# A soft-capped attention and spectral mixing kernel: block sums moved behind the first low parts, a script of its own for the first batch, channel weight blocks split one step ahead

## The chip, the cores and the metric

One core of a Trainium2 chip runs the whole program. The metric is the device time of one execution in microseconds. Three runs of the kernel before took 902.58, 902.90 and 904.99 us, so the median is 902.9 us.

## What is computed

Attention over 8 batches, 12 heads, 448 positions and 64 dimensions per head, with scores capped by a tanh, and behind it a mixing stage on the 768 joined channels, all in float32:

```python
scores = scale * (q @ k.T);  scores = cap * tanh(scores / cap)
x = softmax(scores) @ v                      # per head, heads joined to [b, 448, 768]
theta = x @ w_theta
y = w_tok_r @ (x * cos(theta)) + w_tok_i @ (x * sin(theta))
u = x + y
out = u + max(u @ w_ch, 0)
```

## The kernel before

**Slots.** The 96 heads are handled as 48 pairs. The program walks through slots `s`, and slot `s` computes the scores, tanh and exp of pair `s` and the product of the probabilities with `v` of pair `s - 1`. Slots 0 to 7 (`opening`) do that alone; from slot 8 each slot also carries a sixth of the mixing stage of one batch (`slot`, `part_scripts`). Six slots make a batch: slots 8 to 13 mix batch 0, slots 14 to 19 batch 1, up to batch 6; batch 7 is mixed in the lists of `TAIL` after the attention has ended.

**The mixing stage of a batch** has three products on TensorE (PE), each in three passes of high and low parts: `theta` (names `th`, lines 440 to 442) in rows 0 and 1 of the script, the mixing over positions (`mix`, `mx`, lines 505 to 507) in rows 2 and 3, the channel product (`chan`, `ch`, lines 440 to 442) in rows 4 and 5. Each has six blocks of 128 channels. Between `theta` and `mix`, block by block, VectorE (DVE) folds the angle (`fold`, lines 457 to 459), ScalarE (ACT) takes sine and cosine (`sincos`), DVE multiplies with x (`rotate`, line 468) and transposes within squares (`turn`, line 475), two rounds of DMA through a DRAM tile finish the transposition (`turn`, `back`, lines 477 and 483, issued on SP), ACT makes the high part (`high`, `zh`, line 491) and DVE the low part (`low`, `zl`, line 497). `mix` of a block starts with `zh` and needs `zl` at its third matmul. `gain` (line 511) adds the result to x on DVE, `us` splits it for the channel product.

**Sums of the softmax.** `add_half` adds the exponentials of a pair on DVE into `psz` and reduces them over blocks of 32 keys into `part` (lines 304, 306, 294). On every second pair, the odd ones, it also reduces the last keys of both pairs (`rest`, line 294) and adds those to `part` (line 314). `sums` (event `r`) is a small matmul on `part` (line 368), `invert` (event `inv`) the reciprocal `rq` and a DMA to DRAM, `spread` (event `bc`) four DMAs that bring the factors back, `norm` multiplies x with them.

**Weights.** The blocks of `w_theta`, `w_tok` and `w_ch` arrive as 64-bit words and are split on the chip into high and low float32 parts (`Split`, lines 102 to 135): a load on SP into a staging room, a scaling on ACT (`scale`) or DVE (`vscale`, line 121), and six DVE instructions, plus the cast to the high part on ACT or on DVE (lines 126 to 135). The staging room of `ch` blocks 0, 2 and 4 is `g_sb[0]`, that of 1, 3 and 5 `g_sb[1]`; the same two tiles hold blocks 0 to 2 and 3 to 5 of the rotated values, so a channel block can be loaded only after the low parts of those are made. The table `WEIGHTS` says at which slot and position (`a`, `b`, `c`, for the events `wa`, `wb`, `wc`) a step is loaded (`>`), scaled (`*` on ACT, `#` on DVE) and split (no mark).

**Order.** Everything runs in the order in which it is written, on each engine's own in-order queue; SP issues all DMAs but those of `v`. Nothing is rescheduled. The order inside a slot is the row of `part_scripts`, event by event. In the rows, `SA` and `SB` are the two halves of the scores, `V` the product with `v`, `A`, `B` the two exps, `a`, `b` the two halves of the sums (`a-`, `b-` those of the pair of the slot before), `q` the load of the pair two slots ahead. PSUM accumulators of 512 columns rotate through three buffers.

Of the kernel before, what the change touches and what calls it, by code (L numbers as in the profile page):

```python
# [36 lines left out]
def softcap_attn_then_spectral_mix(ctx, tc, qk2, v, vj, cap, w_theta, w_tok, w_ch, sel, outT):  # L37
# [115 lines left out]
    def weight_steps():  # L153
        for m in range(NJ):
            ms = slice(m * P, (m + 1) * P)
            steps["th", m] = Split(room_g(m), w_theta[m], wth_h[:, :, ms], wth_l[:, :, ms])
            steps["ch", m] = Split(room_g(m), w_ch[m], wch_h[:, :, ms], wch_l[:, :, ms], m not in (2, 4))
# [138 lines left out]
    def add_half(k, half):  # L296
# [5 lines left out]
        if joint(k):  # L302
# [5 lines left out]
            if k % 2 == 1:  # L308
                rest = wk.tile([P, 2 * TB], F32, tag="rest", name=f"rest{k}", bufs=1)
                block_sums(rest, ph)  # L310
                part = parts[k] = state.pop("part")
                for n in range(2):
                    rows = slice(n * D, (n + 1) * D)
                    nc.vector.tensor_tensor(part[rows, n], part[rows, n], rest[rows], op=ALU.add)
# [8 lines left out]
        if k % 2 == 1:  # L323
            parts[k] = state.pop("part")

# [200 lines left out]
    def part_scripts(b):  # L526
        return [row.split() for row in (
# [9 lines left out]
        )]  # L537
# [57 lines left out]
    def slot(s):  # L595
# [6 lines left out]
        def do(e):  # L602
# [28 lines left out]
            if e in ("a-", "b-") and tail:  # L631
                add_half(k, "ab".index(e[0]))
            if e == "norm":
# [92 lines left out]
```

## Time and profile before

| what | value |
|---|---|
| runs | 902.58, 902.90, 904.99 us |
| the profiled execution's own time | 905.26 us |
| its span, first to last instruction | 903.5 us |
| busy: PE, PE weight load, DVE, ACT | 98 %, 73 %, 74 %, 66 % |
| mean granted TensorE clock | 0.991 of full |

The span is the time from the first to the last instruction that the profiler saw; the 1.8 us that the own time has more lie around it. Busy shares are means over the whole span: an engine with 74 % can be the limit in one slot and idle in the next. A matmul's duration is modelled and overlaps its neighbours', so the distance between the starts of two matmuls is the better measure of PE's pace.

### The profile page before, as it was taken

What the parts mean: (1) busy time and instruction counts of PE and PEld (TensorE: products, weight loads), DVE (VectorE), ACT (ScalarE), POOL (GpSimd) and SP (SyncE); (2) the same over time, 40 slices, a digit from 0 to 9 for tenths busy, and PEclk for the clock granted to TensorE, in tenths of its full rate; (3) what the DMA queues carried; (4) which work ended last, traced back from release to release, by engine and by line L of the source; (5) the groups of instructions that cost most, each with busy time, mean ns of one, the idle gap of its engine ahead of it and who ended that gap; (6) DMA issues with size and microseconds to landing.
All of it is one profiled execution on the core that took longest, in us unless ns stands there. A gap on an engine that the chain in (4) does not pass through costs nothing.

```text
span 903.5 us, 12561 instructions
## 1 busy us (share of the span) xinstructions
PE 884.3 (98%) x4848; PEld 660.2 (73%) x4848; DVE 668.7 (74%) x939; ACT 592.2 (66%) x596; POOL 1.1 (0%) x7
## 2 busy tenths in 40 slices
PE   8999989999999999999999999999999999999997
PEld 5333757667787787787777877877877777789997
DVE  5998996996975579756878569765797568864851
ACT  6988775457964687666976479746885568754320
POOL 0000000000000000000000000000000000000000
PEclk9999979999999999999999999999999999999999
DMA  7573176412652237232461225522273233501521
GB/s 262 190 216 123 50 213 203 136 68 73 196 152 84 79 98 214 79 113 84 146 190 52 103 72 164 183 74 83 75 211 111 93 104 115 172 22 50 193 84 64
DMA packets 67339, 112.81 MB, mean 125 GB/s; under 512 B 9672, under 2 KB 49096, under 8 KB 67272
## 3 DMA queue, kind: packets, MB, share of 16 engines
q1 hardware_dynamic: 61656, 102.95, 36.0%
q10 hardware_dynamic: 5616, 8.98, 3.4%
q8 instruction: 40, 0.66, 0.3%
q14 instruction: 27, 0.22, 0.1%
HBM read 76.89 MB, written 33.17 MB: 122 GB/s over the span
## 4 chain that ended last, share of the span: by engine, by line
PE 75%; DVE 10%; ACT 7%; DMA 4%; issue 2%; SPq 1%; DVEq 0%; POOL 0%; POOLq 0%
PE mx L507 8%; PE s L239 8%; PE mx L505 8%; PE mx L506 8%; PE a L336 7%; PE ch L440 6%; PE ch L442 6%; PE ch L441 6%; PE th L440 4%; PE th L442 4%; PE th L441 3%; ACT p L268 3%; PE s L228 2%; DMA g_sb<-turn 2%; DVE g_sb L475 2%; PE a L347 2%
## 5 line engine op out<-in xcount | busy, mean ns | idle before, releaser
L268 ACT ACTIVATE p<-s,qscale 128x1792 f32<-128x1792 f32 (+1 forms) x96 | 166.5, 1734 | 135.6 <-PE s L239 107.1
L507 PE MATMUL mx<-wtk_h,zl 128*128 128x448 f32 x336 | 125.2, 372 | 3.1 <-DVE zl L497 3.1
L505 PE MATMUL mx<-wtk_h,zh 128*128 128x448 f32 x336 | 125.6, 374 | 0.0
L506 PE MATMUL mx<-wtk_l,zh 128*128 128x448 f32 x336 | 124.1, 369 | 0.0
L442 PE MATMUL ch<-us,wch_l 128*128 128x448 f32 x288 | 106.1, 368 | 1.9 <-DVE wch_l L135 1.9
L440 PE MATMUL ch<-us,wch_h 128*128 128x448 f32 x288 | 107.4, 373 | 0.2 <-ACT wch_h L131 0.2
L440 PE MATMUL th<-xs,wth_h 128*128 128x448 f32 x288 | 106.7, 370 | 0.0
L441 PE MATMUL ch<-us,wch_h 128*128 128x448 f32 x288 | 105.8, 367 | 0.0
L442 PE MATMUL th<-xs,wth_l 128*128 128x448 f32 x288 | 105.2, 365 | 0.0
L441 PE MATMUL th<-xs,wth_h 128*128 128x448 f32 x288 | 105.2, 365 | 0.0
L280 ACT ACTIVATE p<-p,cap_sb 128x1792 f32<-128x1792 f32 (+1 forms) x56 | 100.1, 1788 | 0.4
L336 PE MATMUL a<-p,v 128*64 128x448 f32 x480 | 99.0, 548 | 0.0
L497 DVE TENSOR_TENSOR zl<-g_sb,zh 128x896 fp32r<-128x896 f32 x48 | 51.5, 1086 | 33.4 <-ACT zh L491 13.9
L519 DVE SCALAR_TENSOR_TENSOR x<-ch,x 128x448 f32<-128x448 f32 x48 | 29.8, 621 | 58.0 <-PE ch L442 58.0
L507 PEld LDWEIGHTS mx<-wtk_h,zl 128*128 128x128 f32 x336 | 63.9, 190 | 12.0 <-DVE zl L497 6.6
L505 PEld LDWEIGHTS mx<-wtk_h,zh 128*128 128x128 f32 x336 | 64.0, 191 | 10.8 <-issue 3.4
L336 PEld LDWEIGHTS a<-p,v 128*64 128x64 f32 x480 | 30.9, 136 | 51.5 <-issue 43.0
L506 PEld LDWEIGHTS mx<-wtk_l,zh 128*128 128x128 f32 x336 | 64.0, 190 | 5.2
L440 PEld LDWEIGHTS ch<-us,wch_h 128*128 128x128 f32 x288 | 54.5, 189 | 9.3 <-issue 3.1
L491 ACT CAST zh<-g_sb 128x896 fp32r<-128x896 f32 x48 | 44.6, 938 | 25.4 <-DMA g_sb<-turn 9.4
L440 PEld LDWEIGHTS th<-xs,wth_h 128*128 128x128 f32 x288 | 54.1, 188 | 9.2 <-issue 5.1
L442 PEld LDWEIGHTS ch<-us,wch_l 128*128 128x128 f32 x288 | 54.6, 190 | 6.7 <-DVE wch_l L135 2.3
(88 smaller groups left out, 1486.6 us busy)
## 6 DMA issues: line engine op xcount, KB each, us to landing
turn<-g_sb SPq DMA_DIRECT2D x48, 448.0 KB, 3.1
g_sb<-turn SPq DMA_DIRECT2D x192, 112.0 KB, 3.2
qk_sb<-in_qk SPq DMA_DIRECT2D x39, 448.0 KB, 3.5
out_dram<-x SPq DMA_DIRECT2D x48, 224.0 KB, 1.9
bc<-inverse SPq DMA_DIRECT2D x80, 112.0 KB, 3.4
v<-in_vj ACTq DMA_DIRECT2D x20, 256.0 KB, 2.6
g_sb<-in_wth SPq DMA_DIRECT2D x6, 768.0 KB
g_sb<-in_wch SPq DMA_DIRECT2D x6, 768.0 KB, 4.7
```

Of the source, the lines that this page charges most:

```text
L239: nc.tensor.matmul(sp[:, i, hh, :S], kk[k][rows, 1, at : at + P], qq[k][rows, 0, :], start=n == 0, stop=n == 2)
L268: return lambda: nc.scalar.activation(pp[rows, :n], sp[rows, :n, :, :S], AF.Tanh, scale=qscale[rows])
L280: nc.scalar.activation(pp[rows], pp[rows], AF.Exp, scale=cap_sb[rows])
L336: nc.tensor.matmul(acc[hh * D : (hh + 1) * D, :S], va[:, c, hh, :], pt[k, c // 2][:, c % 2, hh, :], start=c == 0, stop=False)
L440: nc.tensor.matmul(acc[:, :S], wh[:, j, ms], t[:, 0, :], start=j == 0, stop=False)
L441: nc.tensor.matmul(acc[:, :S], wh[:, j, ms], t[:, 1, :], start=False, stop=False)
L442: nc.tensor.matmul(acc[:, :S], wl[:, j, ms], t[:, 0, :], start=False, stop=j == NJ - 1)
L491: nc.scalar.copy(zh.rearrange("p c (g t) -> p c g t", g=4), turned(j))
L497: nc.vector.tensor_tensor(zl.rearrange("p c (g t) -> p c g t", g=4), turned(j), zh.bitcast(F32).rearrange("p c (g t) -> p c g t", g=4), op ...
L505: nc.tensor.matmul(acc[:, :S], zh[:, c, :], wtk_h[:, c, :], start=c == 0, stop=False)
L506: nc.tensor.matmul(acc[:, :S], zh[:, c, :], wtk_l[:, c, :], start=False, stop=False)
L507: nc.tensor.matmul(acc[:, :S], zl[:, c, :], wtk_h[:, c, :], start=False, stop=c == NC2 - 1)
```

## The change

1. **Sums in two events.** The part of `add_half` that reduces `ph` (`rest`) and adds it to `part` becomes a function `add_ends` with events of its own, `c` and `c-` (for the pair of the slot before).
2. **Rows 1 and 2 of the script (slots 9, 15, 21, ...).** Row 1: `b` moves behind `fold5` (the last event). Row 2: `c-` stands behind `low1`, and `r inv` moves from before `SB` to behind `mix0`. In rows 3 and 5 `c` stands right behind `b`, and the events that are dropped from the rows do nothing there.
3. **The first batch has rows 1 and 2 of its own.** `fold4`, `fold5`, `b-` and `c-` move into slot 10, `r inv bc` there behind `mix1`, and the weight events move.
4. **Channel blocks.** Block 1 is split at (9, `b`) instead of (9, `a`); block 2 is loaded at (10, `b`) and split at (10, `c`), where before it was loaded at (10, `c`) and split at (11, `c`); block 4 goes from (12, `c`) to (11, `c`), block 5 from (13, `b`) to (12, `c`), scaled on DVE. The cast of blocks 1 and 5 goes from ACT to DVE.

```diff
-            steps["ch", m] = Split(..., m not in (2, 4))
+            steps["ch", m] = Split(..., m in (0, 3))
...
-        (8, "b"): "tk5", (8, "c"): "*tk6 *ch1", (9, "a"): "tk6 ch1", (10, "c"): ">ch2", (11, "c"): ">ch3 #ch2 ch2 >ch4", (12, "b"): "*ch3 ch3 >ch5", (12, "c"): "#ch4 ch4", (13, "b"): "*ch5 ch5",
+        (8, "b"): "tk5", (8, "c"): "*tk6 *ch1", (9, "a"): "tk6", (9, "b"): "ch1", (10, "b"): ">ch2", (10, "c"): "#ch2 ch2 >ch4", (11, "c"): ">ch3 #ch4 ch4",
+        (12, "b"): "*ch3 ch3 >ch5", (12, "c"): "#ch5 ch5",
...
             block_sums(state["part"][:, k % 2], psz)
-            if k % 2 == 1:
-                rest = ...; block_sums(rest, ph)
-                ...
+    def add_ends(k):
+        if k % 2 == 0 or not joint(k):
+            return
+        rest = wk.tile([P, 2 * TB], F32, tag="rest", name=f"rest{k}", bufs=1)
+        block_sums(rest, ph)
+        part = parts[k] = state.pop("part")
+        for n in range(2):
+            rows = slice(n * D, (n + 1) * D)
+            nc.vector.tensor_tensor(part[rows, n], part[rows, n], rest[rows], op=ALU.add)
...
-            "SA fold2 norm sincos0 V wa x v r SB tB prep wb rotate0 turn0 rotate1 turn1 back0 rotate2 turn2 back1 q"
-            " A th3 fold3 a B b th4 fold4 back2 wc th5 fold5",
-            "SA high0 low0 high1 sincos1 low1 V wa x v r inv SB tB prep q wb rotate3 turn3 high2 rotate4 turn4 back3 mix0 gain0 low2"
-            " rotate5 turn5 back4 back5 bc A B wc mix1 gain1 mix2",
+            "SA fold2 norm sincos0 V x v SB tB prep rotate0 turn0 rotate1 turn1 back0 rotate2 turn2 back1 q"
+            " A th3 fold3 a B th4 fold4 back2 th5 fold5 b",
+            "SA high0 low0 high1 sincos1 low1 c- V x v SB tB prep q rotate3 turn3 high2 rotate4 turn4 back3 mix0 r inv gain0 low2"
+            " rotate5 turn5 back4 back5 bc A B mix1 gain1 mix2",
...
+        if b == 0:
+            rows[1] = ("SA fold2 norm sincos0 V wa x v SB tB rotate0 turn0 rotate1 turn1 wb back0 rotate2 turn2 back1 q"
+                       " A B th3 fold3 a th4 back2 th5")
+            rows[2] = ("SA high0 low0 fold4 fold5 high1 sincos1 low1 b- c- V x v SB tB q rotate3 turn3 high2 rotate4 turn4 back3 mix0 gain0 low2"
+                       " rotate5 turn5 back4 back5 A B wb mix1 gain1 wc r inv bc mix2")
```

How the queues move, at three places. The first is DVE at the end of slot 10 of batch 0. Before, from `gain1` to the low part of block 3:

```order
L511 TENSOR_TENSOR x_256<-mx_1_1004,x_256 128x448
L304 TENSOR_TENSOR psz<-p_0_901 128x896
L511 TENSOR_TENSOR x_304<-mx_2_1027,x_304 128x448
L497 TENSOR_TENSOR zl_3_1063<-g_sb_94,zh_3_1061 128x896
L497 TENSOR_TENSOR zl_4_1076<-g_sb_94,zh_4_1074 128x896
```

Now, from behind `gain1`, the same stretch:

```order
L121 TENSOR_SCALAR g_sb_93<-g_sb_93 128x768
L126 TENSOR_SCALAR g_sb_93<-g_sb_93 128x768
L127 SCALAR_TENSOR_TENSOR g_sb_93<-g_sb_93 128x768
L128 TENSOR_SCALAR g_sb_93<-g_sb_93 128x768
L129 SCALAR_TENSOR_TENSOR g_sb_93<-g_sb_93 128x768
L133 CAST wch_h<-g_sb_93 128x6x128
L134 TENSOR_TENSOR g_sb_93<-g_sb_93,wch_h 128x768
L135 TENSOR_TENSOR wch_l<-g_sb_93 128x6x128
L411 RECIPROCAL rq_1026<-r_1024 56x32
L305 TENSOR_TENSOR psz<-p_0_889 128x896
L516 TENSOR_TENSOR x_304<-mx_2_1036,x_304 128x448
L502 TENSOR_TENSOR zl_3_1072<-g_sb_94,zh_3_1070 128x896
```

The eight instructions that scale and split channel block 2 (`g_sb_93` is the staging room) and the reciprocal `rq` now stand ahead of the low part of block 3.

The second is SP in slot 10 of batch 0. Before, from the last turn of the batch on:

```order
L477 DMA turn_5_985<-g_sb_94 128x896
L483 DMA g_sb_94<-turn_4_952 32x4x224 x4
L483 DMA g_sb_94<-turn_5_985 32x4x224 x4
L417 DMA bc_995<-inverse_934 64x448 x2
L417 DMA bc_998<-inverse_934 64x448 x2
L114 DMA g_sb_93<-in_wch 128x1536
L190 DMA qk_1091<-in_qk 128x896
```

Now:

```order
L482 DMA turn_5_979<-g_sb_94 128x896
L488 DMA g_sb_94<-turn_4_946 32x4x224 x4
L488 DMA g_sb_94<-turn_5_979 32x4x224 x4
L114 DMA g_sb_93<-in_wch 128x1536 x2
L413 DMA inverse_1028<-rq_1026 56x32
L422 DMA bc_1030<-inverse_1028 64x448 x2
L422 DMA bc_1033<-inverse_1028 64x448 x2
L191 DMA qk_1100<-in_qk 128x896
```

The load of channel block 2 still stands right behind the eight DMAs that bring back blocks 4 and 5; block 4's load follows it, and the four `bc` DMAs and the load of the next pair stand behind both.

The third is DVE around the first low parts of the later batches, here batch 1 (slots 15 and 16). Before:

```order
L306 TENSOR_TENSOR psz<-psz,p_1_1647 128x896
L294 TENSOR_REDUCE part_1581<-psz 128x28
L294 TENSOR_REDUCE rest_1704<-ph 128x28
L314 TENSOR_TENSOR part_1581<-part_1581,rest_1704 64x28 x2
...
L497 TENSOR_TENSOR zl_0_1776<-g_sb_93,zh_0_1774 128x896
L497 TENSOR_TENSOR zl_1_1782<-g_sb_93,zh_1_1778 128x896
L406 RECIPROCAL rq_1803<-r_1801 56x32
...
L511 TENSOR_TENSOR x_558<-mx_0_1840,x_558 128x448
L497 TENSOR_TENSOR zl_2_1863<-g_sb_93,zh_2_1830 128x896
```

Now:

```order
L307 TENSOR_TENSOR psz<-psz,p_1_1647 128x896
L295 TENSOR_REDUCE part_1581<-psz 128x28
L502 TENSOR_TENSOR zl_0_1772<-g_sb_93,zh_0_1770 128x896
L502 TENSOR_TENSOR zl_1_1778<-g_sb_93,zh_1_1774 128x896
L295 TENSOR_REDUCE rest_1780<-ph 128x28
L329 TENSOR_TENSOR part_1581<-part_1581,rest_1780 64x28 x2
...
L411 RECIPROCAL rq_1858<-r_1856 56x32
L516 TENSOR_TENSOR x_558<-mx_0_1834,x_558 128x448
L502 TENSOR_TENSOR zl_2_1863<-g_sb_93,zh_2_1824 128x896
```

The first two low parts now stand ahead of `rest` and its two additions (and the second half of the sums behind both folds), while the set of instructions ahead of the third low part, `zl_2`, is the same as before.

## Rows read from the trace of the kernel before

**Rows 1.** The page: busy time of the engines, and the chain that ended last by engine.
```profile
PE 884.3 (98%) x4848; PEld 660.2 (73%) x4848; DVE 668.7 (74%) x939; ACT 592.2 (66%) x596; POOL 1.1 (0%) x7
...
PE 75%; DVE 10%; ACT 7%; DMA 4%; issue 2%; SPq 1%; DVEq 0%; POOL 0%; POOLq 0%
```
**Rows 2.** Who waited for whom, PE's own list: line, what it waited for, us in total, times, longest.
```profile
PE mx L507 <- DVE zl L497: 3.1, 7, 0.7
```
**Rows 3.** Timeline of PE, batch 0, slots 10 and 11: start, us, line, operands, count, and in brackets the idle time before it and its releaser.
```profile
123.53 0.37 PE L368 MATMUL r<-sel_sb,part 128*56 128x32 f32 x2 [2.96 <-DVE part L314]
...
127.35 0.74 PE L507 MATMUL mx<-wtk_h,zl 128*128 128x448 f32 x1 [0.70 <-DVE zl L497]
...
128.63 0.57 PE L507 MATMUL mx<-wtk_h,zl 128*128 128x448 f32 x1
129.00 0.57 PE L505 MATMUL mx<-wtk_h,zh 128*128 128x448 f32 x1
...
134.03 0.36 PE L505 MATMUL mx<-wtk_h,zh 128*128 128x448 f32 x1
134.23 0.36 PE L506 MATMUL mx<-wtk_l,zh 128*128 128x448 f32 x1
...
142.63 1.74 PE L249 MATMUL s<-qk_sb 64*64 64x448 f32 x16
...
148.88 0.36 PE L507 MATMUL mx<-wtk_h,zl 128*128 128x448 f32 x1
```
**Rows 4.** Timeline of PE, batch 0, slot 13: the first matmuls of channel block 5.
```profile
192.21 0.47 PE L440 MATMUL ch<-us,wch_h 128*128 128x448 f32 x1 [0.16 <-ACT wch_h L131]
...
194.79 0.74 PE L442 MATMUL ch<-us,wch_l 128*128 128x448 f32 x1 [1.91 <-DVE wch_l L135]
```
**Rows 5.** Stretches of 4 us: length, busy us and instructions of PE, PEld, DVE, ACT, POOL, then the granted clock of PE, the DMA share and GB/s.
```profile
120.00:124.00 4.00, 1.04 (x14) 0.43 (x10) 3.87 (x6) 0.94 (x1) 0.00 (x0) 0.89 0.97 257
124.00:128.00 4.00, 3.30 (x12) 1.25 (x13) 3.86 (x8) 3.65 (x4) 0.00 (x0) 0.50 0.65 138
128.00:132.00 4.00, 4.00 (x13) 3.52 (x12) 3.28 (x5) 3.97 (x5) 0.00 (x0) 0.50 0.55 167
132.00:136.00 4.00, 4.00 (x18) 3.68 (x17) 3.18 (x4) 2.35 (x3) 0.00 (x0) 0.83 0.67 246
...
192.00:196.00 4.00, 1.94 (x6) 1.42 (x6) 3.96 (x5) 3.72 (x4) 0.00 (x0) 0.85 0.12 48
196.00:200.00 4.00, 4.00 (x16) 3.32 (x17) 3.93 (x6) 2.16 (x5) 0.00 (x0) 0.73 0.30 115
```
**Rows 6.** Timeline of DVE, batch 0, slots 9 to 11: first instruction of the split of token block 6, the low parts 0 and 1, `rotate3`, `turn4`, `gain0`, `turn5`.
```profile
102.19 0.39 DVE L126 TENSOR_SCALAR swk_t<-swk_raw 128x448 int32<-128x448 int32 x1
...
126.21 2.09 DVE L497 TENSOR_TENSOR zl<-g_sb,zh 128x896 fp32r<-128x896 f32 x2
...
129.24 1.09 DVE L468 TENSOR_TENSOR g_sb<-g_sb,x 128x896 f32<-128x896 f32 x1 [0.68 <-ACT g_sb L464]
...
132.48 1.11 DVE L475 STREAM_TRANSPOSE g_sb<-g_sb 128x896 f32<-128x896 f32 x1
134.23 0.62 DVE L511 TENSOR_TENSOR x<-mx,x 128x448 f32<-128x448 f32 x1 [0.64 <-PE mx L507]
...
137.13 1.11 DVE L475 STREAM_TRANSPOSE g_sb<-g_sb 128x896 f32<-128x896 f32 x1
```
**Rows 7.** Timeline of DVE, batch 0: the scaling that begins the split of channel block 2, its cast, the `norm` behind it, and in slot 12 the reciprocal `rq`.
```profile
161.06 0.56 DVE L121 TENSOR_SCALAR g_sb<-g_sb 128x768 f32<-128x768 f32 x1
...
164.71 0.56 DVE L133 CAST wch_h<-g_sb 128x768 fp32r<-128x768 f32 x1
...
167.17 1.15 DVE L421 TENSOR_TENSOR x<-bc,x 128x448 f32<-128x448 f32 x2
...
170.38 0.34 DVE L406 RECIPROCAL rq<-r 56x32 f32<-56x32 f32 x1
```
**Rows 8.** Timeline of SP's DMA queue, batch 0, slot 10: start and length of issue of `turn5`, `back4` and `back5`, the `bc` DMAs, and the load of channel block 2.
```profile
138.27 0.34 SPq L477 DMA_DIRECT2D turn<-g_sb  x1
138.71 4.11 SPq L483 DMA_DIRECT2D g_sb<-turn  x8
142.86 2.39 SPq L417 DMA_DIRECT2D bc<-inverse  x4
145.30 0.58 SPq L114 DMA_DIRECT2D g_sb<-in_wch  x1
```
**Rows 9.** The loads of weight blocks (line 114): time from issue to landing, and the sizes of the channel blocks' loads.
```profile
DMA to landing us min/median/max: 4.4/4.5/5.0
...
g_sb<-in_wch SPq DMA_DIRECT2D x6, 768.0 KB, 4.7
```
**Rows 10.** Timelines of DVE and PE, batch 1 (slot 16) and batch 2 (slot 22): the first low part is waited for, and the third low part and the matmul that needs it.
```profile
241.17 0.47 PE L507 MATMUL mx<-wtk_h,zl 128*128 128x448 f32 x1 [0.40 <-DVE zl L497]
...
248.69 1.07 DVE L497 TENSOR_TENSOR zl<-g_sb,zh 128x896 fp32r<-128x896 f32 x1
...
249.95 0.37 PE L507 MATMUL mx<-wtk_h,zl 128*128 128x448 f32 x1
...
354.97 1.07 DVE L497 TENSOR_TENSOR zl<-g_sb,zh 128x896 fp32r<-128x896 f32 x1
...
356.10 0.48 PE L507 MATMUL mx<-wtk_h,zl 128*128 128x448 f32 x1
```

More of the change, by code (lines that the diff above doesn't have):

```diff
@@ L156, in weight_steps @@
             steps["th", m] = Split(room_g(m), w_theta[m], wth_h[:, :, ms], wth_l[:, :, ms])
-            steps["ch", m] = Split(room_g(m), w_ch[m], wch_h[:, :, ms], wch_l[:, :, ms], m not in (2, 4))
+            steps["ch", m] = Split(room_g(m), w_ch[m], wch_h[:, :, ms], wch_l[:, :, ms], m in (0, 3))
         for c in range(NC2):
@@ L307, in add_half @@
             block_sums(state["part"][:, k % 2], psz)
-            if k % 2 == 1:
[L309 to L314, printed above, removed]
             return
@@ L526, in part_scripts @@
     def part_scripts(b):
-        return [row.split() for row in (
+        rows = [
             "SA V wa x v r inv SB tB prep q bc wb A th0 fold0 a B th1 fold1 b wc th2",
[8 rows of a table removed]
-        )]
[8 rows of a table added]
+        ]
+        if b == 0:
[3 more added lines that the diff above has]
+                       " rotate5 turn5 back4 back5 A B wb mix1 gain1 wc r inv bc mix2")
+        return [row.split() for row in rows]
     TAIL = (
@@ L632, in do @@
                 add_half(k, "ab".index(e[0]))
+            if e == "c" and live:
+                add_ends(s)
+            if e == "c-" and tail:
+                add_ends(k)
             if e == "norm":
```

8 rows, old and new, of tables (rows, x) are left out of this document.

## The prediction, made before the changed kernel was run

> **What bounds the kernel now.** I read the page first. PE is busy for 98 % of the span and carries three quarters of the chain that ended last [rows 1], so a change of order pays only where PE stands still, or runs at a lower clock because it stood still. PE's own list of waits and its timeline show where that is. In batch 0, `r` waits 2.96 us for `part`, and the third matmul of `mix0` waits 0.70 us for the first low part [rows 3]. In slot 13, channel block 5 waits 0.16 us for its high part and 1.91 us for its low part [rows 4]. The first low part of a batch is waited for seven times, 3.1 us together; that is the 0.70 us and six waits of 0.40 us in batches 1 to 6 [rows 2, 10]. Third, the granted clock in stretches of 4 us [rows 5]: behind the wait for `part` it is at its lower level, 1.2 GHz, for 0.9 + 4 + 4 + 1.4 = 10.2 us (a share of 0.89 means that 11/50 of a stretch was low, and so on), behind the wait for channel block 5 for 1.2 + 2.2 = 3.4 us. Matmuls start 0.37 us apart at the lower level and 0.20 us apart at 2.4 GHz [rows 3], so a microsecond at the lower level loses 1 - 0.203/0.374 = 0.46 us. Last, DVE's timeline: in batch 0 DVE has no gap from 102.19 us to the end of the low parts, which is 126.21 + 2.0 = 128.2 us [rows 6]. There DVE is the real limit, and PE's waits are its shadow.
>
> **Channel block 5: a gain of 3.6 us.** Its split moves from slot 13 into slot 12, some 10 us before it is needed. Both waits go, 2.1 us [rows 4], and with them the low clock behind, 3.4 x 0.46 = 1.5 us [rows 5]. Slot 12 loses the split of block 4 and gains that of block 5, so DVE's work there is about the same. If block 5's load, which is issued behind the split of block 3, makes DVE wait a little, this costs nothing while PE still has blocks 2 to 4 in front of it.
>
> **Batches 1 to 6: nothing, where 2.4 us look possible.** `rest` and its two additions, 1.5 us of DVE, move behind the first two low parts, and the 0.40 us go at `mix0`. But the third low part has the same instructions ahead of it as before, only in another order, and DVE is busy all the way. In batch 1 it ends at 248.69 + 1.07 = 249.76 us, and PE reads it at 249.95; in batch 2 it ends at 356.04, and PE reads it at 356.10 [rows 10]. PE has 0.1 to 0.2 us to spare. Arriving 0.40 us earlier, it waits for `low2` in place of `low0`: that is what is late next. The moved folds now wait some 0.1 us for ACT, because the sums no longer stand between them. I take 0, between -1 us (0.2 us in each of six batches) and +0.6 us. `r` behind `mix0` has no cost of its own: its matmuls run either way, and `rq` stands behind `turn4`, when `mix0` is long done.
>
> **Batch 0, up to `mix2`: better.** In slots 9 and 10 DVE makes `rotate0` to `turn1` before the split of channel block 1, and the low parts before the sums. `mix0` should start near 122 us in place of 125.5, without the wait for `part` and without the low clock behind. The cast of block 1 goes from ACT to DVE, + 0.6 us [rows 7]. But everything up to `turn5` is the same DVE work: 128.2 - 102.2 = 26.0 us that held no gap, plus 0.6 for the cast; then `rotate3` to `turn4`, 4.3 us (129.24 to 133.5); `gain0` and `low2`, 1.6; `rotate5` and `turn5`, 2.2 [rows 6]. From 102.2 that is 136.9 us. A gap for sine, cosine or a returning block is likely; I take 137.2 for the end of `turn5` (137.0 to 138.5), where it was 138.2. So 3 us that PE wins up to `mix1` are lost again at `mix2`, which needs `low2`; slot 10 ends only some 2 to 3 us earlier.
>
> **Batch 0, the split of channel block 2: a loss of 8.8 us.** This is the step that decides. The split was in slot 11, behind `us2`, where DVE had room. Now its eight instructions stand in DVE's queue between `gain1` and `low3`, and DVE works in order. Its load cannot be early either: on SP it stands behind `back5`, which waits for `turn5`. In the trace the eight returns behind `turn5` are issued 142.86 - 138.27 = 4.6 us after it [rows 8]. I take the same distance, so the load is issued at 137.2 + 4.6 = 141.8 us. The loads of weight blocks land 4.4 to 5.0 us after their issue, 4.5 in the median [rows 9]: 146.3 us. DVE is done with `gain1` near 138 and stands still for 8 us. Then follow the scaling and the split, 167.17 - 161.06 = 6.1 us [rows 7], to 152.4; `rq`, 0.3 [rows 7]; the first half of the sums, 1.0; `gain2`, 0.55; `low3`, 1.1 (such instructions start that far apart [rows 6]). The low part of block 3 is ready at 155.4 us. PE gets to the matmul that needs it near 146 and waits some 9 us. In the trace it ran at 148.88 us without a wait [rows 3]: a delay of **6.5 us** that has the gain in slot 10 in it already. The bounds: 137.0, 4.4 and 3.5 us for a landing without other traffic give 153.8, or +4.9; 138.5, 4.8 and 5.0 give 157.3, or +8.4.
>
> After such a wait the clock will be low. It stayed low for 3.4 us where matmuls ran on without gaps, for 10.2 us where a second wait followed [rows 5]. `mix3` runs on without gaps, but the wait is longer; I take 5 us, 5 x 0.46 = **2.3 us**, between 1.5 and 4.6. What hides none of it: from `mix3` to slot 13 PE had no wait, so the delay stays.
>
> Queued behind the waiting scaling on DVE are also the sums of pair 10; the tanh of the second half of pair 11 needs the buffer they read, so ACT is held until 153.7 us. Its results are not needed before slot 12. On SP, block 4's load, the four `bc` DMAs and the load of pair 13 wait too, until 157 us; the `norm` that needs them stands behind another split, near 174, and pair 13 is needed in slot 13.
>
> The Trainium skill ("DMA: Bandwidth & Descriptors", Rules for kernel authors) tells to issue a DMA early, compute, and wait for it late. The changed row does the reverse with block 2, and the rule speaks against it; the 8 us that DVE stands still are the same thing in rows. The page's fit for a transfer (Anatomy of one DMA), 2.0 us and the bytes at 436 GB/s, was measured on another issue path; as an estimate from it, 768 KB take 3.8 us. By it the loss would be 0.7 us smaller; rows 9 are measured here, and decide.
>
> **The sum.** + 6.5 + 2.3 - 3.6 + 0 = + 5.2 us. The profiled execution took 905.26 us, so it would be 910.5; the median of the runs shown is 902.9, 2.4 us lower, and I put the change on that: **908.1 us**. With the bounds: + 4.9 + 1.5 - 3.6 - 1.0 = + 1.8, and + 8.4 + 4.6 - 3.6 + 0.6 = + 10.0.
>
> **Rivals.**
> *The split of block 2 does not hold DVE up (faster).* If the data are there when DVE comes, DVE goes from `gain1` at 137.8 through 6.1 + 0.3 + 1.0 + 0.55 + 1.1 us to 146.9 us: 2.0 us before the 148.88. Less 3.6 for block 5 and with 1 us of low clock this is -4.6, or 898 us. It decides from a landing before about 140 us. For it: the row and the table keep load and split apart by two positions. Against: `mix1 gain1` between them are no DVE work, and SP cannot issue the load before `turn5` has landed [rows 8].
> *The low clock lasts as long as after the first wait.* 10.2 us at 0.46 in place of 2.3 gives + 7.6, 910.5 us. For it: the wait would be three times as long. Against: `mix3` to `mix5` have no gaps.
> *The later batches keep their 0.40 us.* If `low2` comes earlier, since ACT starts `sincos1` earlier, 2.4 us are won: + 2.8, 905.7 us. Against: DVE, and not ACT, sets `low2` [rows 10].
> *The change is hidden.* If the first batch gains all it can (2.96 + 0.70 + 10.2 x 0.46 = 8.4 us) and the wait at `mix3` takes that back whole, only block 5 is left with a loss of some 3 us in slot 11: near 902.9. I see no row for a delay that small.
>
> **How the numbers follow.** Runs of this kernel lie 0.3 % apart, 2.7 us; less than that is no change. The forecast gets 0.60, the long low clock 0.14, the later batches 0.10, the hidden change 0.07, the rival that ends faster 0.09. The forecast's own spread (904.7 to 912.9) and the third rival put some 0.14 within 2.7 us; so faster 0.09, same 0.16, slower 0.75. The range takes in the forecast with most of its bounds and the second and third rival: 904.0 to 912.5.
>
> **What would show it.** Right: DVE idle for about 8 us before line 121 near 138 to 146 us, released by the load; PE idle for some 9 us before the third matmul of `mix3`, released by `zl`; the clock low there and for some us after; no wait for channel block 5 and full clock in slot 13; no `r` wait for `part`; six waits of 0.2 to 0.4 us at `mix2` in place of `mix0`. Wrong: a load of block 2 that lands before 141 us, or a `mix3` that starts before 150.

## The result, and the profile after

The change makes the kernel slower: 912.6 us in the median (912.33 to 914.19), where the kernel before, run beside it, took 903.6 (902.58 to 904.99). The ratio is 1.0102, with a 95 % interval of 1.0083 to 1.0122. Forecast were 908.1 us and a range up to 912.5: the side was right, the size was not, + 9.0 us in place of + 5.2. The traced execution took 912.4 us, with a span of 910.2. Here and below times are medians, while a ratio with its interval leaves out the few executions that were far longer than the rest, and is not the quotient of the two medians.

The page of the changed kernel, beside [rows 1]: PE has lost 3 us of busy time, and its part of the chain that ended last falls from 75 to 66 %; DVE's rises from 10 to 19 %.

```profile
PE 881.1 (97%) x4848; PEld 657.8 (72%) x4848; DVE 670.4 (74%) x942; ACT 589.1 (65%) x593; POOL 1.1 (0%) x7
...
PE 66%; DVE 19%; ACT 8%; DMA 4%; issue 3%; SPq 1%; DVEq 0%; ACTq 0%
```

PE's own list of waits, which answers to [rows 2] (line 512 is the old line 507, line 510 the old 505; us in total, times, longest):

```profile
PE mx L512 <- DVE zl L502: 13.4, 8, 10.7
...
PE mx L510 <- DVE x L516: 3.7, 1, 3.7
```

The waits of `r` for `part` and of channel block 5 [rows 3, 4] are gone. In their place stand one wait of 10.72 us for a low part and one of 3.75 us for a result of DVE's line 516, `gain0`. PE's timeline in batch 0, slots 10 and 11, puts both in their places (start, us, line, operands, count, and in brackets the idle time and its releaser):

```profile
130.22 0.29 PE L373 MATMUL r<-sel_sb,part 128*56 128x32 f32 x2
134.26 0.71 PE L510 MATMUL mx<-wtk_h,zh 128*128 128x448 f32 x1 [3.75 <-DVE x L516]
...
135.16 0.74 PE L512 MATMUL mx<-wtk_h,zl 128*128 128x448 f32 x1
...
140.25 1.74 PE L250 MATMUL s<-qk_sb 64*64 64x448 f32 x16
...
146.29 0.36 PE L511 MATMUL mx<-wtk_l,zh 128*128 128x448 f32 x1
157.37 0.74 PE L512 MATMUL mx<-wtk_h,zl 128*128 128x448 f32 x1 [10.72 <-DVE zl L502]
...
160.89 0.57 PE L512 MATMUL mx<-wtk_h,zl 128*128 128x448 f32 x1
161.26 0.41 PE L510 MATMUL mx<-wtk_h,zh 128*128 128x448 f32 x1
161.51 0.37 PE L511 MATMUL mx<-wtk_l,zh 128*128 128x448 f32 x1
```

The long wait is the third matmul of `mix3`. Behind it matmuls start 0.37 us apart until 161.3 us, then 0.20. DVE's timeline, to be read against [rows 6, 7], tells why:

```profile
118.36 1.09 DVE L305 TENSOR_TENSOR psz<-p 128x896 f32<-128x896 f32 x1
120.77 1.09 DVE L502 TENSOR_TENSOR zl<-g_sb,zh 128x896 fp32r<-128x896 f32 x1 [1.31 <-ACT zh L496]
...
134.04 1.07 DVE L502 TENSOR_TENSOR zl<-g_sb,zh 128x896 fp32r<-128x896 f32 x1
...
136.14 1.11 DVE L480 STREAM_TRANSPOSE g_sb<-g_sb 128x896 f32<-128x896 f32 x1
137.18 0.58 DVE L516 TENSOR_TENSOR x<-mx,x 128x448 f32<-128x448 f32 x1
148.39 0.56 DVE L121 TENSOR_SCALAR g_sb<-g_sb 128x768 f32<-128x768 f32 x1 [10.62 <-DMA g_sb<-in_wch]
...
154.50 0.34 DVE L411 RECIPROCAL rq<-r 56x32 f32<-56x32 f32 x1
...
155.71 0.60 DVE L516 TENSOR_TENSOR x<-mx,x 128x448 f32<-128x448 f32 x1
156.24 2.07 DVE L502 TENSOR_TENSOR zl<-g_sb,zh 128x896 fp32r<-128x896 f32 x2
```

DVE is done with `gain1` at 137.8 us and stands still for 10.62 us, until block 2's load has landed; split, `rq`, `psz` and `gain2` follow, and only then `low3`. On SP's queue (start and length of issue) the load comes 5.7 us behind `turn5`, where [rows 8] gave 4.6:

```profile
137.28 0.34 SPq L482 DMA_DIRECT2D turn<-g_sb  x1
137.72 5.21 SPq L488 DMA_DIRECT2D g_sb<-turn  x8
142.97 11.99 SPq L114 DMA_DIRECT2D g_sb<-in_wch  x2
```

ACT's timeline shows two waits that come with it: the first theta copy of block 3 waits for the end of block 1's split, because both use one staging room, and the second tanh of slot 11 waits for the block sums behind the split of block 2.

```profile
115.03 0.54 ACT L456 ACTIVATE g_sb<-th 128x448 f32<-128x448 f32 x1 [3.34 <-DVE wch_l L135]
...
119.81 0.92 ACT L496 CAST zh<-g_sb 128x896 fp32r<-128x896 f32 x1
...
155.88 1.75 ACT L269 ACTIVATE p<-s,qscale 128x1792 f32<-128x1792 f32 x1 [10.00 <-DVE psz L305]
```

The granted clock in stretches of 4 us, columns as in [rows 5]: it falls in slot 10 (a short piece behind the wait for `gain0`), falls again while PE stands at `mix3`, and is full in slot 13, where channel block 5 starts near 202 us.

```profile
132.00:136.00 4.00, 1.74 (x4) 1.29 (x5) 3.97 (x5) 1.93 (x2) 0.00 (x0) 0.76 0.67 244
136.00:140.00 4.00, 4.00 (x18) 3.60 (x17) 1.73 (x3) 0.00 (x0) 0.00 (x0) 0.82 0.79 243
...
148.00:152.00 4.00, 0.00 (x0) 0.00 (x0) 3.47 (x5) 0.00 (x0) 0.00 (x0) 0.89 0.01 3
152.00:156.00 4.00, 0.00 (x0) 0.00 (x0) 3.93 (x7) 0.12 (x1) 0.00 (x0) 0.50 0.16 20
156.00:160.00 4.00, 2.63 (x7) 2.38 (x8) 3.97 (x5) 3.31 (x2) 0.00 (x0) 0.50 0.45 178
160.00:164.00 4.00, 4.00 (x18) 3.63 (x18) 1.55 (x2) 0.87 (x2) 0.00 (x0) 0.83 0.64 178
...
200.00:204.00 4.00, 4.00 (x22) 3.70 (x21) 3.98 (x5) 0.66 (x2) 0.00 (x0) 1.00 0.47 119
```

In batch 1 (slot 16) the wait stands at the third low part now, and not at the first as in [rows 10]:

```profile
256.10 0.47 PE L512 MATMUL mx<-wtk_h,zl 128*128 128x448 f32 x1 [0.34 <-DVE zl L502]
```

The opening's length varies by up to 1.3 us between the traces here, so pieces are compared from the first theta matmul on. The table is worked out from PE's timelines: us from there to the first score matmul of slots 11, 12 and 14, and from slot 14 to the span's end.

| traced execution | first theta matmul at | slot 11 | slot 12 | slot 14 | rest |
|---|---|---|---|---|---|
| kernel before | 87.29 | 55.34 | 74.04 | 112.51 | 703.7 |
| changed kernel | 86.42 | 53.83 | 85.31 | 119.59 | 704.2 |
| split 2 behind `low4` | 86.03 | 54.02 | 77.29 | 112.28 | 704.3 |
| load 2 ahead of `turn5` | 86.22 | 54.11 | 81.76 | 116.05 | 705.2 |
| before, block 5 early | 86.98 | 55.14 | 73.83 | 109.57 | 703.7 |
| batch-0 rows alone | 86.76 | 54.37 | 73.06 | 111.55 | 705.6 |
| block 5 behind `ch2` | 86.98 | 54.36 | 73.04 | 108.36 | 704.4 |
| `low2`, `gain0` earlier | 87.23 | 50.95 | 69.63 | 105.59 | 701.7 |
| no load of block 2 | 86.78 | 54.36 | 73.30 | 107.64 | 704.4 |
| before, wait filled | 86.56 | 52.60 | 71.29 | 108.19 | 703.7 |

So the changed kernel wins 1.5 us up to slot 11, is 11.3 us behind at slot 12, gets 4.2 back in slots 12 and 13, and loses 0.5 in the rest: + 7.6 us between the two traces. The shorter opening takes 0.9 off, and the time outside the span is 0.4 longer (2.2 us against 1.8): + 7.1, which is 912.4 less 905.26.

### The profile page after: what moved, and what is told of

Its sections match the earlier page's. It is cut to its first block, busy times and chain, and to the rows that moved or that the text cites. A ratio compares the mean times of both kernels' runs of the same rounds, so it can differ in the third digit from the quotient of the medians.

```text
span 910.2 us, 12546 instructions
## 1 busy us (share of the span) xinstructions
PE 881.1 (97%) x4848; PEld 657.8 (72%) x4848; DVE 670.4 (74%) x942; ACT 589.1 (65%) x593; POOL 1.1 (0%) x7
## 4 chain that ended last, share of the span: by engine, by line
PE 66%; DVE 19%; ACT 8%; DMA 4%; issue 3%; SPq 1%; DVEq 0%; ACTq 0%
PE s L240 8%; PE ch L445 7%; PE a L341 7%; PE ch L447 6%; PE ch L446 6%; PE mx L512 5%; PE mx L510 5%; PE mx L511 5%; PE th L445 4%; PE th L447 3%; PE th L446 3%; DVE g_sb L473 3%; DVE g_sb L480 3%; DVE zl L502 2%; ACT p L269 2%
## 5 line engine op out<-in xcount | busy, mean ns | idle before, releaser
L445 PEld LDWEIGHTS ch<-us,wch_h 128*128 128x128 f32 x288 | 54.1, 188 | 8.7 <-issue 3.1
L446 PEld LDWEIGHTS ch<-us,wch_h 128*128 128x128 f32 x288 | 54.1, 188 | 4.4
```

Source lines behind the costliest of these rows:

```text
L445: nc.tensor.matmul(acc[:, :S], wh[:, j, ms], t[:, 0, :], start=j == 0, stop=False)
L446: nc.tensor.matmul(acc[:, :S], wh[:, j, ms], t[:, 1, :], start=False, stop=False)
```

## The experiments

Ratios are to the kernel before, run on the same chip. The diffs show the changed parts of lines alone; `...` marks code that is left out.

**The split of block 2 behind `low4`** (from the changed kernel).
```diff
- (10, "b"): ">ch2", (10, "c"): "#ch2 ch2 >ch4",
+ (10, "b"): ">ch2", (11, "a"): "#ch2 ch2 >ch4",
- "SA a- gain2 high3 low3 V wa x v high4 low4 SB ...
+ "SA a- gain2 high3 low3 V x v high4 low4 wa SB ...
```


> The changed kernel, with one thing undone: the scaling and the split of channel block 2 (and the load of block 4 behind it) stand behind low4 in slot 11 and no longer between gain1 and low3; its load stays where the change put it. Theory (the split holds DVE, DVE holds mix3): low3 is ready near 145.5 us, the third matmul of mix3 runs near 146.5 us without a wait, in place of 157.4. That is 10.9 us, and the low clock behind the wait goes too, some 4 us x 0.46 = 1.9 us: 912.6 - 12.8 = 899.8 us (898.5 to 901.5). Rival A (something else in the change delays mix3 as well, such as the block sums or zh): mix3 still waits for over 2 us, 903 us or more. Rival B (the stall moves: low5 now stands behind the split and mix5 waits for it 2 to 3 us, with a low clock behind): 902.5 to 904.

905.7 us, ratio 1.0024 (1.0011 to 1.0037). `mix3` no longer waits, but the gain on the changed kernel is some 7 us and not 12.8: the mechanism is that of rival B, though the time is 1 to 2 us above its 902.5 to 904. `low5` stands behind the split and `mix5` waits for it; slot 12 comes 3.3 us later than in the kernel before. So the split was what held `mix3`, but put in this place it makes `low5` late.
```profile
157.68 0.60 PE L512 MATMUL mx<-wtk_h,zl 128*128 128x448 f32 x1 [2.72 <-DVE zl L502]
```

**The load of block 2 ahead of `turn5`** (from the changed kernel).
```diff
- gain0 low2 rotate5 turn5 back4 back5 A B wb mix1 ...
+ gain0 low2 wb rotate5 turn5 back4 back5 A B mix1 ...
```


> The changed kernel with block 2's load issued right behind low2, ahead of turn5 and of the eight returns on SP; the split stays between gain1 and low3. Theory (the load comes late because of its place on SP): it is issued near 135.5 us in place of 142.97, lands 4.5 to 6 us later (it shares the queue with turn5 and the returns), so DVE waits 2 to 4 us in place of 10.6, low3 is ready near 151 and mix3 waits some 4.5 us in place of 10.7: 912.6 - 6.3 = 906.3 us (904 to 908). Rival (the transfers themselves are the limit, 0.9 MB of turns and returns in front of or beside the load): it lands no earlier than 146, or the returns of block 3 come later and hold high3 instead: 909 to 912.

908.2 us, ratio 1.0044 (1.0028 to 1.0059): about 5 us won, less than expected. The load is issued 7.1 us earlier and lands 4.3 us earlier, 8.2 us after its issue. The eight returns now take 8.9 us to issue; for 4.2 us of that SP stands between the first four and the last four until `turn5`, issued behind the load, has landed (0.9 us in the changed kernel). Both theories have a part: the place on SP costs, and so do the transfers beside it. SP first, with its wait between 136 and 148 us, then DVE:
```profile
135.90 0.38 SPq L114 DMA_DIRECT2D g_sb<-in_wch  x1
...
137.86 8.90 SPq L488 DMA_DIRECT2D g_sb<-turn  x8
...
SPq L488 <- DMA turn<-g_sb: 4.2, 1, 4.2
```
```profile
144.07 0.56 DVE L121 TENSOR_SCALAR g_sb<-g_sb 128x768 f32<-128x768 f32 x1 [6.52 <-DMA g_sb<-in_wch]
```

**Block 5 early, alone** (from the kernel before; scaled and cast on DVE, as in the changed kernel).
```diff
- (12, "c"): "#ch4 ch4", (13, "b"): "*ch5 ch5",
+ (12, "c"): "#ch4 ch4 #ch5 ch5",
```


> The kernel before, with channel block 5's scaling (on DVE) and split moved from slot 13 to the end of slot 12, behind block 4's; nothing else. Theory: the two waits of slot 13 go (2.07 us) and 3.4 us of low clock behind them (x 0.46 = 1.5 us): 903.6 - 3.6 = 900.0 us (899 to 901). Rival A (DVE now has three splits in slot 12; the norms and the additions behind them are late, and PE waits for a PSUM buffer of ch2 or ch3 instead): 902.5 or more. Rival B (only the waits count, the low clock is paid elsewhere): 901.5.

902.4 us, ratio 0.9984 (0.9972 to 0.9995): 1.4 us, not 3.6. Between the two traces slots 12 and 13 are 2.7 us shorter; why the medians show half of that is taken up below, under "Wrong, second". Rival A has part of it: a wait of 1.3 us for a PSUM buffer, held by an addition that is queued behind the third split.
```profile
PE ch L440 <- DVE x L519: 1.3, 1, 1.3
```

**The new order in batches 1 to 6, alone** (the kernel before with `add_ends` and the new rows for those batches; batch 0 and the weight blocks as before).

> The kernel before, with the changed order of the block sums in batches 1 to 6 alone; batch 0 and the weight blocks as before. Theory: the wait of 0.40 us goes from mix0 to mix2 in each of the six batches and nothing is won: 903.6 us (902.8 to 904.3). Rival A (low2 comes earlier too, 6 x 0.40 us are won): 901.2. Rival B (mix2 waits longer than mix0 did, or r behind mix0 costs something): 904.5 to 906.

904.6 us, ratio 1.0006 (0.9994 to 1.0018): nothing, as forecast. In this trace too the wait in batch 1 stands at `mix2`:
```profile
249.43 0.47 PE L511 MATMUL mx<-wtk_h,zl 128*128 128x448 f32 x1 [0.41 <-DVE zl L501]
```

**The rows of batch 0 alone** (the changed kernel, channel blocks 2, 4 and 5 split at their old places; not shown: the cast of block 5 goes back to ACT, and `wb` back into the last row. Block 2's load keeps its new place).
```diff
- (10, "c"): "#ch2 ch2 >ch4", (11, "c"): ">ch3 #ch4 ch4",
+ (11, "c"): ">ch3 #ch2 ch2 >ch4",
- (12, "b"): "*ch3 ch3 >ch5", (12, "c"): "#ch5 ch5",
+ (12, "b"): "*ch3 ch3 >ch5", (12, "c"): "#ch4 ch4", (13, "b"): "*ch5 ch5",
```


> The changed kernel with channel blocks 2 to 5 split where the kernel before split them (block 2 behind us2 in slot 11, block 4 in slot 12, block 5 in slot 13); so of the change only the order of the rows stays. Theory: slot 10 ends 2.0 us earlier (140.05 us in the run with the split behind low4 against 142.12 in the kernel before with block 5 early), DVE has room in slot 11 as before, so mix3 and mix5 don't wait and the 2 us stay; in those executions of the kernel before whose clock is low for a shorter time there is less to win, so 1 us (0.5 to 2.0) under the kernel before, and some 10 us under the changed kernel. Rival A (the rows themselves cost time further on, in slots 11 to 13): as fast as before or slower. Rival B (low5 is late even without the split in front of it): mix5 waits for over 1 us.

904.5 us beside 906.3, ratio 0.9986 (0.9975 to 0.9998): 1.3 us won, as expected. Slot 11 comes 1.0 us earlier, and slots 12 and 14 keep that. Against this kernel the changed one loses 1.0102 - 0.9986, some 10.5 us, by the new places of the three splits, with the load of block 4 and the cast of block 5.

**Block 1's split ahead of `rotate1`** (from the changed kernel).
```diff
- rotate0 turn0 rotate1 turn1 wb back0 ...
+ rotate0 turn0 wb rotate1 turn1 back0 ...
```


> The changed kernel with the split of channel block 1 two positions earlier, behind turn0 in place of turn1; nothing else. Theory (the split of block 1 holds ACT's theta copies of block 3 by its staging room, ACT then holds zh0, and DVE stands still for 1.3 us before the first low part): the copies start some 2.2 us earlier, the gap before the first low part goes, turn5, block 2's load and mix3 all come 0.9 to 1.3 us earlier: the changed kernel less 1.1 us. Rival (the gap has another reason, such as the landing of the returned block): the gap stays over 1 us and the time is the same.

913.9 us beside 906.3, ratio 1.0084 (1.0062 to 1.0105): not to be told from the changed kernel. ACT's hold shrinks from 3.34 to 1.23 us, yet the gap ahead of the first low part stays, 1.62 us: `back0` stands on SP behind `turn1`, which is later now, so the returned block is late. The hold was real, but a second wait of the same size stood behind it. ACT, then DVE:
```profile
112.85 0.55 ACT L456 ACTIVATE g_sb<-th 128x448 f32<-128x448 f32 x1 [1.23 <-DVE wch_l L135]
...
120.04 0.94 ACT L496 CAST zh<-g_sb 128x896 fp32r<-128x896 f32 x1 [1.90 <-DMA g_sb<-turn]
```
```profile
121.01 1.09 DVE L502 TENSOR_TENSOR zl<-g_sb,zh 128x896 fp32r<-128x896 f32 x1 [1.62 <-ACT zh L496]
```

**Block 5 behind `ch2`** (from the run with the batch-0 rows alone; not shown: the cast of block 5 is on DVE, and `wb` leaves the last row).
```diff
- (12, "c"): "#ch4 ch4", (13, "b"): "*ch5 ch5",
+ (12, "c"): "#ch4 ch4", (12, "d"): "#ch5 ch5",
- ... b wc norm ch2"
+ ... b wc norm ch2 wd"
```


> As the run with the batch-0 rows alone, but block 5 is scaled and split at the end of slot 12, behind ch2's own addition, not in slot 13. Theory: the additions of ch0 to ch2 are no longer queued behind the third split of slot 12 (the 1.3 us wait of the run with block 5 early), so both waits of slot 13 and the low clock behind them go: 3.2 us under the run with the batch-0 rows alone (2.5 to 3.6), 4 us under the kernel before. Rival (DVE reaches block 5's split too late, since ch2 ends near 181 us, and the wait for its low part stays in part): under 1.5 us won.

901.9 us beside 906.3, ratio 0.9960 (0.9945 to 0.9975): 2.6 us under the batch-0 rows alone. With the additions ahead of the third split no matmul of slots 12 and 13 waits for a PSUM buffer; 0.9 us of wait for block 5's low part is left.

**`low2` and `gain0` earlier** (from the run above).
```diff
- SB tB prep q rotate3 turn3 high2 rotate4 turn4 back3 mix0 r inv gain0 low2 ...
+ SB tB prep q mix0 rotate3 turn3 gain0 rotate4 high2 low2 turn4 back3 r inv ...
  (batch 0)
- SB tB q rotate3 turn3 high2 rotate4 turn4 back3 mix0 gain0 low2 ...
+ SB tB q mix0 gain0 rotate3 turn3 high2 low2 rotate4 turn4 back3 ...
```


> As the run with block 5 behind ch2, and in every batch gain0 and low2 stand earlier on DVE: in batch 0 gain0 ahead of rotate3 and low2 ahead of rotate4, in the others gain0 ahead of rotate4 and low2 ahead of turn4. Theory: mix2 of batch 0 waits 1 us for gain0 or low2 in place of 3.7 (2 to 2.7 us won), and the six waits of 0.34 to 0.41 us at mix2 go (2.2 us won): 4.5 us under the run with block 5 behind ch2 (3 to 5). Rival A (turn4 is now later and high4 or low4 takes the wait over): only the 2 us of batch 0, or less. Rival B (DVE now waits for zh2, so all behind it comes later): no gain or a loss.

896.6 us beside 906.3, ratio 0.9900 (0.9882 to 0.9918): faster than both kernels, and some 5.4 us under the run above where 3 to 5 were expected. Slot 11 comes 3.4 us earlier than in the run above, and the rest behind slot 14 is 2.7 us shorter: the small waits of the later batches are gone but for one of 0.4 us. Three waits for a low part are left in the whole kernel:
```profile
PE mx L512 <- DVE zl L502: 1.8, 3, 1.0
```

**No load of block 2** (from the changed kernel).
```diff
     def load(self):
         raw, self.t = self.room()
-        nc.sync.dma_start(raw.bitcast(I32), self.src)
+        if self is not steps["ch", 2]:
+            nc.sync.dma_start(raw.bitcast(I32), self.src)
```


> The changed kernel without the load of channel block 2: its scaling and split run in the same place over what stands in the staging room, so block 2's weights are not the given ones; all else is the same. It parts the wait for the load from the work of the split. Theory (the wait costs, the place in DVE's order alone does not): DVE goes on behind gain1 at 137.8 us without standing still, 6.1 + 0.3 + 1.0 + 0.55 + 1.1 us later low3 is ready, 146.9 us, and mix3 waits 0.3 to 0.6 us for it in place of 10.7: the changed kernel less 12 us, 900 to 901.5 us, or 3 us under the kernel before. Rival (6 us of split in front of low3 hurt in any case, since ACT and the block sums are held as well): mix3 or mix5 still wait, and the time is 903 us or more.

900.6 us beside 904.5, ratio 0.9954 (0.9939 to 0.9969): 13 us under the changed kernel, as the theory had it. DVE does the same work in the same order without standing still, and the third matmul of `mix3` runs at 147.39 us without a wait. Slot 12 comes within 0.3 us of where it does in the run with the batch-0 rows alone. So the order costs next to nothing; the wait for the data is the loss. This run also leaves out the transfer itself and what it held up on SP, which it does not price apart; the run with the split behind `low4` kept the load, and `mix3` had no wait there either.
```profile
138.05 0.56 DVE L122 TENSOR_SCALAR g_sb<-g_sb 128x768 f32<-128x768 f32 x1
...
145.91 2.07 DVE L503 TENSOR_TENSOR zl<-g_sb,zh 128x896 fp32r<-128x896 f32 x2
```

**The kernel before, twice more.**

> The kernel before, unchanged, to see its two kinds of execution: of 30 runs on one chip those with a mean clock of 0.991 took 904.7 us in the mean, those with 0.995 took 902.0 us. Theory: the difference is the length of the low clock behind the wait for the block sums in batch 0. If this execution has 0.991 or 0.992, the clock there is low for some 10 us as in the profile shown; if it has 0.995 or 0.996, for some 3.5 us, with the same waits, and slot 11 begins 2.5 to 3 us earlier. Rival: the waits differ, or the low clock lies elsewhere.

> The kernel before, unchanged, once more, with the same expectation as the run before it: the wait for the block sums is 3 us in both kinds, and the low clock behind it lasts some 10 us in an execution at 0.991 or 0.992 and some 3.5 us in one at 0.995 or 0.996.

905.0 and 906.95 us, with mean clocks of 0.991 and 0.992: both are of the kind already traced, so how the other kind differs was not seen. Here the low clock again lasts 10 us behind a wait of 3.2 us (the first of the two):
```profile
120.00:124.00 4.00, 0.95 (x6) 0.57 (x10) 3.82 (x7) 1.45 (x2) 0.00 (x0) 0.73 0.99 278
124.00:128.00 4.00, 3.31 (x13) 1.56 (x6) 3.91 (x7) 3.81 (x4) 0.00 (x0) 0.50 0.53 131
128.00:132.00 4.00, 4.00 (x12) 3.51 (x12) 3.50 (x5) 3.61 (x5) 0.00 (x0) 0.50 0.50 160
132.00:136.00 4.00, 4.00 (x21) 3.72 (x20) 3.31 (x4) 2.81 (x3) 0.00 (x0) 0.99 0.73 257
```

**The wait for the block sums filled with matmuls** (from the kernel before).
```diff
                 state["r"] = psM.tile([P, 512], F32, tag="m", name=f"r{k}")
+                for _ in range(12 if k == FIRST + 1 else 0):
+                    nc.tensor.matmul(state["r"][:32, :CP], ones_sb, ones_sb[:, :1].broadcast_to([CP, CP]), ...)
```


> The kernel before, with 12 small matmuls (ones into the tile of r, overwritten by r itself; 0.21 us each, as the 16 recorded in 1.75 us of the opening, so some 2.5 us) in front of r of pairs 8 and 9: TensorE works through most of the 3 us in which it waited for the block sums. Nothing comes earlier by it, only the clock is tested. Theory (the low clock behind this wait is 10.2 us in one kind of execution and shorter in the other; it is worth 0.46 us per us): the low stretch goes or shrinks to 3.4 us, slot 11 begins up to 3 us earlier although DVE is as late as before, and the two kinds draw together: the median falls by 1.5 to 3.5 us against the kernel before, and no execution is left at 0.991. Rival A (what follows is set by DVE's low parts in any case, so the clock costs nothing there): the same time, within 0.7 us. Rival B (such small matmuls do not keep the clock up): the low stretch stays at 10.2 us and the time is the same.

903.0 us beside 902.8, ratio 1.0004 (0.9989 to 1.0020). No theory holds whole. None is left at 0.991, but the median did not fall, and the executions did not draw together: of 12, three have a mean clock of 0.999 (900.4 us in the mean), four 0.995 (902.9), five 0.993 (905.3). But the traced one is of the first kind: though it waits 0.62 and 2.09 us in slot 10 and 1.9 us in slot 13, its clock is full in every stretch of batch 0's mixing, and slot 11 comes 2.7 us earlier, slot 14 4.3 us earlier than in the kernel before. So the low clock has about that price (rival A falls), as far as one execution of each of two programs can show it. One and the same program has executions at 0.999 and at 0.993, 4.9 us apart; where the clock is low in the latter was not traced. PE, then the stretches:
```profile
119.55 2.53 PE L369 MATMUL r<-ones_sb 112*32 112x112 f32 x24
122.70 0.29 PE L370 MATMUL r<-sel_sb,part 128*56 128x32 f32 x2 [0.62 <-DVE part L314]
...
126.60 0.47 PE L509 MATMUL mx<-wtk_h,zl 128*128 128x448 f32 x1 [2.09 <-DVE zl L499]
```
```profile
124.00:128.00 4.00, 1.91 (x9) 1.44 (x10) 3.74 (x7) 3.97 (x4) 0.00 (x0) 1.00 0.60 137
128.00:132.00 4.00, 4.00 (x22) 3.70 (x21) 3.52 (x4) 3.97 (x6) 0.00 (x0) 1.00 0.53 170
```
The Trainium skill ("TensorE: Matmul & The Clock Gate", Part 1) says of a kernel's start that the number of matmuls at the lower level differs from run to run. The mean clocks of the 12 executions differ too, but they do not say where in them the clock is low.

## Why the prediction was right in kind and wrong in size

**Right: where the time goes.** The split of block 2 stands in DVE's queue, waits there for its load, and holds `low3` and `mix3`. Without the load the 13 us are back (0.9954 against 1.0102), with the same order of work. Rival 1, that the split does not hold DVE up, is what that run shows: it needs the data, and they came at 148.4 us and not before 140. The Trainium skill ("DMA: Bandwidth & Descriptors", Rules for kernel authors) tells to wait late for a DMA. The changed kernel (1.0102) and the run with the split behind `low4`, which waits later (1.0024), agree with it.

**Right: the small terms.** Batches 1 to 6 give nothing (1.0006), and the wait moves from `mix0` to `mix2`. The reason given, that `low2` is late next, is borne out by the run with `low2` and `gain0` earlier, where these waits go; its rest is 2.7 us shorter, of which 1 to 2 us can be the difference between any two traces. Slots 12 and 13 of the changed kernel are 4.2 us shorter; forecast were 3.6 for block 5. Here block 4 is split a slot earlier too: with block 5 alone moved, the gain was 2.7 us between the traces. The gain up to slot 11 was put at 2 to 3 us and is 1.5. In batch 0 PE stands at `mix2` for `gain0`, and not for `low2`, as I wrote: `r` now takes the third PSUM buffer between `mix1` and `mix2`, so `mix2` needs the buffer of `mix0`. But `low2`, next on DVE, was ready at 134.04 + 1.07 = 135.11 us, and the matmul that needs it started at 135.16: it would have held PE about as long. The forecast had no low clock behind this wait; the two stretches from 132 to 140 us hold 3.4 us of it.

**Wrong, first: the size of the wait in "the split of channel block 2".** Its terms, on the time scale of the kernel before (0.87 us added for the opening): `turn5` ended at 138.1 us, forecast 137.2. The missing 0.9 us is the gap of 1.31 us ahead of the first low part; I had counted the cast that went from ACT to DVE, but not that ACT's copies wait for the room that block 1's split occupies. What this hold alone is worth stays open: where it was shortened, a late returned block took its place. The load was issued 5.7 us behind `turn5`, forecast 4.6; 0.6 us of the difference is SP's wait for `turn5` to land, 0.9 us where it was 0.3. It landed 5.4 us later, forecast 4.5. Together that is 2.9 us, and `mix3`'s third matmul is 9.4 us late in place of 6.5. The two DMA terms were one row and a median of the kernel before; in the three runs with the load right behind the returns that show both they are 5.0 to 5.7 and 5.2 to 5.4 us, never 4.6 and 4.5. The larger figure for the landing stood in the trace: [rows 9] hold three landings, and the longest of them is block 2's own, issued at 145.30 us [rows 8] (line 114, from 144 to 148 us):
```profile
DMA to landing us min/median/max: 5.0/5.0/5.0
```
In the five other traces of runs that keep this load in its old place it took 5.1 to 6.6 us. The 3.5 us of the lower bound has no row; no load of a channel block landed in under 4.0 us. That bound also adds up to 154.0 us, not 153.8. By the estimate of 3.8 us from the Trainium skill ("DMA: Bandwidth & Descriptors", Anatomy of one DMA) the miss would have been larger still; the measurements decide. The clock behind the wait went as forecast: 161.3 - 157.4 = 3.9 us at the lower level while matmuls ran, 1.8 us lost, forecast 2.3. By the traces, then, + 7.1 us at slot 14 for + 5.2.

**Wrong, second: "2.4 us lower, and I put the change on that".** This cost the other half. The forecast for the traced execution was 910.5 us and it took 912.4; the shift to the median made 908.1 of it. The traced execution of the kernel before lay above its median, with a mean clock of 0.991, and its kind of execution is the longer one: of 77 executions of that kernel in these studies 40 have a mean clock of 0.991 or 0.992, 29 one of 0.995 or 0.996, and on one chip the groups at 0.991 and 0.995 took 904.7 and 902.0 us. The changed kernel's four executions lie at 0.990 to 0.993, and its trace at its median. The sum was made against an execution with 13.6 us of low clock [rows 5] and credits the change with taking it away; an execution that loses less to the clock has less to win. So + 5.2 could not be moved onto the median unchanged, and the times shown, 902.6, 902.9 and 905.0, already hinted at two groups. Block 5 early, alone, shows the same: its traced execution took 3.0 us less than that of the kernel before, while its ratio is worth 1.4. The filled wait shows what lies between such groups in one program: 5 us. That the clock alone makes this difference is argued from the mean clocks, and not shown by a trace of the shorter kind.

**Left open.** Which of the low stretches is shorter in the other half of the executions was not traced. The rest behind slot 14 varies by 1 to 2 us between traces with the same order of work there. And the time outside the span is 2.0 to 2.2 us in the runs with block 5 early, 1.8 to 1.9 in the others; nothing here tells why.

## What to carry to other kernels

Before a step that waits for a load is moved ahead in an engine's queue, follow the load back to what frees its room and to its place in the issuing queue: a load that cannot start earlier turns an early step into a standstill for all that is queued behind it. Take its landing from that very load and not from a median over others, 5.0 us and not 4.5 here, and leave room above it: the same load took 5.0 to 6.6 us in six traces. And before a trace is set against a median, compare the clock of the traced execution with that of the timed ones: a low clock that only some executions have is no sure gain. What paid most here was moving the two instructions that the next matmuls wait for, `gain0` and `low2`, ahead of others that are needed later: 0.6 % on top of the 0.4 % that the new rows of batch 0 and block 5 behind `ch2` gave.

## What the runs showed of the hardware that was not expected

- One program, the one with the filled wait, has executions at mean clocks from 0.993 to 0.999, which take 905.3 to 900.4 us; in the traced one, at 0.999, the clock never falls in batch 0's mixing. There a wait of 2.09 us passed without a low clock, where waits of 2.96 and 0.70 us in the kernel before had 10.2 us of it.
- 13.6 us at the lower level [rows 5] cost 4.3 us up to slot 14, by the traces of the kernel before and of the filled wait, not the 6.3 us that 0.46 us each would make. The 3.4 us in slot 13 cost 1.6, as reckoned; the 10.2 us in slot 10 cost 2.7 in place of 4.7: part of them lay beside DVE's work, and `mix0` with a full clock only waited longer for its low part, 2.09 us in place of 0.70.
- The load of channel block 2, 768 KB, landed 5.0 us after its issue in the kernel before, 5.0 to 6.6 us in the six traces with its old place, 5.2 to 5.4 us right behind eight returns, and 8.2 us when it was issued ahead of `turn5` and the returns. The issue of those eight returns took 4.1 us before and 8.9 us behind the load, with 0.3 and 4.2 us of wait for `turn5` to land in it.
